# The opening of a fused gated-attention and token-mixer kernel: a z piece cast later, warm-up products, one block computed instead of turned, score pairs split between engines, loads at other times

## The chip, the cores and the metric

The kernel runs on one core of a Trainium2 chip. The time is that of one launch, in device microseconds, taken as the median of several runs; lower is better. A core has five engines that run their own instruction queues: TensorE (PE: matrix products; its weight loads are listed as PEld), VectorE (DVE), ScalarE (ACT), GpSimd (POOL) and SyncE (SP, which here only issues DMAs). They meet through semaphores. PSUM, the accumulator memory, has eight banks.

## What is computed

Two modules in a row, for each of 8 batches of 3200 tokens:

```
scores = z @ z.T / S                      # z: 3200 x 64
attn   = maximum(scores, 0) ** 2
x      = u * (attn @ v)                   # u, v: 3200 x 256

wq, wk = x @ w_q, x @ w_k                 # 256 x 64 each
mixed  = (wq @ wk.T / 8) @ x              # no softmax: wq @ (wk.T @ x)
out    = maximum(mixed, 0) @ w_out        # 256 x 256
```

Inputs and output are float32; the kernel multiplies in float16 and accumulates in float32.

## The kernel before

**Tiles.** A batch has 25 tiles of 128 tokens (the rows of scores) and seven groups of columns, six of 512 and one of 128. For each group the kernel makes the scores of all 25 tiles against the group's columns, squares their positive part, and accumulates the product with v in four PSUM banks (`acc00` to `acc11`; two halves of the group, two row halves of the product).

**Pairs.** Scores are made two tiles at a time (`use_pair`, `scores`): two products on the two row halves of the array, into one of two PSUM slots (`ps`). `first_stage` takes them out with a relu, on ACT or DVE, 1024 columns at once, into a float32 tile `g`; `second_stage` squares `g` into a float16 tile `at`, on ACT or POOL. There are 14 `at` buffers. The slot is free for a later pair, projection or other use when the relu is done.

**Blocks that are turned.** The score matrix is symmetric. For two groups near each other `is_turned` is true, and the block made for the earlier group is transposed by a DMA from SP (`turn`, tile `tt` or `ttl`) and used again for the later one, where no scores are made. An `at` buffer is free only when its turned blocks have been read.

**The order.** The program's order is made while it is built, by a scheduler with its own clocks for four engines (`clock`), for SP (`sp_at`) and for the DMA (`dma_at`). Its main loop takes, step by step, a pair of scores, an extra (projection, heads, mix, output) or one accumulation step (`acc_step`, `open_rows`), whichever its clocks find ready. `at_time` and `move` queue loads and DMAs for a planned time. `choose` and `squares` pick the engine of a relu and a square. Each engine then executes its queue in that order, waiting on semaphores: the planned times themselves are in no instruction, only the order is.

**The opening.** Batch 0's z comes in four pieces (`ZCH`: tiles 0 to 3, 12 to 17, 18 to 24, 4 to 11), is cast to float16 twice side by side (`cast_first`), turned by TensorE (`turn_first`) and copied to `zT`. v of batch 0 comes in five loads from POOL's queue (`load_first_v`), converted to float16 on the way. All four z pieces use buffers of the pool for x. The loads of u, of w_out and of the other weights follow on SP; nothing ahead of the first of them waits for a compute engine. The first pieces' casts are spread over DVE, ACT and POOL; those of the last piece are on POOL and DVE, and the DVE one is in the queue ahead of the first relu.

**Later.** When the two halves of a group are accumulated, `gate` takes them out of PSUM (ACT copy, DVE addition), multiplies with u on POOL, and SP transposes the result to `xT_sb` for the projections (L371), which accumulate toward `hs`. Mix (L436) and output products (L463) of a batch are placed among the next batch's accumulations. `batch_begun` plans the loads and transposes of the next batch's z and the loads of its v. The tail after the main loop ends the last batch.

Of the kernel before, what the change touches and what calls it, by code (L numbers as in the profile page):

```python
# [16 lines left out]
def kernel(  # L17
# [36 lines left out]
    NEARBY = 8  # L54

# [53 lines left out]
    def cast_first(c, parts=(0, 1)):  # L109
# [5 lines left out]
            (nc.gpsimd.tensor_copy, nc.vector.tensor_copy),  # L115
        ][c]
        for half, cast in enumerate(casts):
            if half in parts:
                cast(out=zd0[:, n0 : n0 + nn, half, :], in_=z32[n0][:])

    def turn_first(c):
        n0, nn = ZCH[c]
        tp = acc_tile(1 - c // 2, c % 2, "ztp", FP16)
# [4 lines left out]
        clock[PE] += 0.14 * nn  # L128
# [4 lines left out]
        z_at[c] = give(ACT if on_act else DVE, ready, 0.2 + 0.065 * nn)  # L133
# [38 lines left out]
    wo32 = {}  # L172

    def load_weights():
        wo32[0] = px.tile([P, ND, D], FP32, tag="x_sb", name="wo32")
        loads = [(wo32[0][:], moe_w_out.rearrange("(c p) e -> p c e", p=P))]
        for r in range(2):
            for w32, w in ((wq32, moe_w_q), (wk32, moe_w_k)):
                loads.append((w32[top(r), :, :], w.rearrange("(c p) h -> p c h", p=dh)))
        for half in range(2):  # L180
            loads.append((wk2[:, :, half, :], moe_w_k.rearrange("(c p) h -> p c h", p=P)))
        for i, (t, w) in enumerate(loads):
            move(18.0 + i, 26.0 + i, 0.65, 0.5, lambda t=t, w=w: nc.sync.dma_start(out=t, in_=w))

    def cast_weights():
# [3 lines left out]
        nc.gpsimd.tensor_copy(out=wo[:], in_=wo32[0][:])  # L189
# [3 lines left out]
    def is_turned(gi, gj):  # L193
# [4 lines left out]

    tiles, ends = [], {}
    for b in range(B):  # L200
        for gi in range(NG):
            near = [t for t in range(NT) if is_turned(gi, group_of(t))]
            own = [
                t for t in range(NT) if t not in near and not is_turned(group_of(t), gi)
            ]
            if b == 0 and gi == 0:
                order = own + near
# [30 lines left out]
    def first_stage(p, sc, on_act):  # L238
        g = pg.tile([P, 2, W], FP32, tag="g", name="g")
        for hs, w in pieces(p):  # L240
# [11 lines left out]
    def second_stage(p, g, on_act):  # L252
        at = pat.tile([P, 2 * W], FP16, tag="at", name="at")
        at0 = 0
        for hs, w in pieces(p):
# [8 lines left out]
        for tile_ in tiles[2 * p : 2 * p + 2]:  # L264
# [3 lines left out]
            if is_turned(gi, gj):  # L268
# [268 lines left out]
    keys_at, out_of, turned_at, z_at = {}, {}, {}, {}  # L537
# [50 lines left out]
    def cold():  # L588
        return 2.0 if clock[PE] < 11.0 else 1.0
# [9 lines left out]
    def use_pair():  # L599
# [12 lines left out]
    def squares():  # L612
        while pending and pending[0][0] <= clock[PE] + 0.3:
# [3 lines left out]
            done = give(ACT, ready, 1.06) if on_act else give(POOL, ready, 1.9)  # L617
            for (b, gi, gj, _, nn, _, _), turn in second_stage(p, g, on_act):
# [108 lines left out]

    def batch_begun(b, t):
        if b + 1 < B:
            t += 6 if b == 0 else 0  # L730
            at_time(t + 6, lambda: (load_z(b + 1), push(3.0)))
            for half in range(2):
                at_time(
                    t + 18 + 3 * half,
                    lambda half=half: (double_z(b + 1, half), give(DVE, clock[PE], 0.98)),
                )
            for i in range(5):
                move(t + 24 + 6 * i, t + 40 + 6 * i, 1.28, 1.05, lambda i=i: turn_z(b + 1, i))
            for i in range(5):
                at_time(t + 20 + 13 * i, lambda i=i: (load_v(b + 1, 5 * i, 5), push(2.5)))  # L740
# [43 lines left out]
    def open_rows():  # L784
# [8 lines left out]
        if b == 0 and gi == 0:  # L793
            ready = [t for t in ready if v_at[t] <= clock[PE]]
# [4 lines left out]
        if len(take) < want:  # L799
            if closing and len(left) - len(take) < 4:  # L800
                take = take[: len(left) - 4]
# [231 lines left out]
```

## Time and profile before

| | us |
|---|---|
| median of three runs | 787.96 (787.84 to 788.57) |
| the profiled execution | 789.18 |
| its span, first to last instruction | 787.2 |
| TensorE busy | 766.2 |
| POOL busy | 638.5 |
| ACT busy | 542.1 |
| DVE busy | 504.1 |

The profile is one execution. Its page gives the busy time of each engine, the chain of work that ended last, and groups of instructions by source line, with what the engine waited for ahead of them. Views of the trace give the same for any stretch of the span. Busy times of engines overlap; an engine's idle time counts only where the others have nothing to do meanwhile.

### The profile page before, as it was taken

How to read it: one execution, taken by the hardware profiler on the slowest of the kernel's cores; microseconds unless marked ns; L12 is line 12 of the kernel's file. 1: busy time of each engine (PE TensorE's matmuls, PEld its weight loads, DVE VectorE, ACT ScalarE, POOL GpSimd, SP SyncE). 2: the span in 40 equal slices, each digit the busy share in tenths (PEclk: the TensorE clock that was granted, in tenths of full speed). 3: DMA queues.
4: the chain of work that ended last, by engine and by line, in shares of the span. 5: the costliest groups of instructions: out<-in, count | busy, mean ns of one | idle time of the engine just before them, and what ended most of it. 6: DMA issues, size and time to landing. Idle time of an engine off the chain costs nothing.

```text
span 787.2 us, 28217 instructions
## 1 busy us (share of the span) xinstructions
PE 766.2 (97%) x12373; PEld 661.6 (84%) x12373; DVE 504.1 (64%) x514; ACT 542.1 (69%) x646; POOL 638.5 (81%) x524
## 2 busy tenths in 40 slices
PE   6989999999999999999998999999999999999996
PEld 4879999887899888988887887988879988898884
DVE  5655768564687566775575666777576665666635
ACT  5757678768687767867676765776667766777534
POOL 7969597887888877898687998789778788988961
PEclk9999999999999999999999999999999999999999
DMA  8999999999999999999989999999979999779616
GB/s 196 145 175 167 166 175 176 184 181 168 214 174 180 201 192 192 195 178 205 188 159 158 213 183 176 180 196 202 207 175 172 154 211 229 177 115 213 146 56 213
DMA packets 308522, 141.38 MB, mean 180 GB/s; under 512 B 287152, under 2 KB 290096, under 8 KB 308400
## 3 DMA queue, kind: packets, MB, share of 16 engines
q1 hardware_dynamic: 301488, 123.42, 83.2%
q0 software_dynamic: 6768, 15.98, 15.3%
q8 instruction: 96, 1.57, 0.8%
q14 instruction: 26, 0.21, 0.1%
q10 hardware_dynamic: 144, 0.20, 0.1%
HBM read 59.64 MB, written 26.21 MB: 109 GB/s over the span
## 4 chain that ended last, share of the span: by engine, by line
PE 91%; DMA 3%; DVE 2%; ACT 1%; issue 1%; POOL 0%; SPq 0%; DVEq 0%; POOLq 0%; ACTq 0%
PE acc L302 66%; PE sc L223 12%; PE fo L463 6%; PE qk L371 3%; DMA xT_sb<-x_sb 3%; PE qk L408 2%; PE mx L436 1%; DVE g L246 1%; DMA z<-in_z_dram 1%; POOL at L261 0%; ACT at L259 0%; ACT g L242 0%; DVE fo L486 0%; PE hd L408 0%; DVE both L319 0%
## 5 line engine op out<-in xcount | busy, mean ns | idle before, releaser
L302 PE MATMUL acc<-v_sb,at 64*128 64x256 f16 x7312 | 495.3, 270 | 3.4 <-ACT at L259 2.5
L261 POOL TENSOR_TENSOR at<-g 128x1024 f16<-128x1024 f32 (+1 forms) x244 | 449.3, 1854 | 56.8 <-DVE g L246 50.6
L246 DVE TENSOR_SCALAR g<-sc 128x1024 f32<-128x1024 f32 (+2 forms) x321 | 376.0, 1189 | 138.1 <-PE sc L223 133.0
L302 PEld LDWEIGHTS <-at 64*128 64x128 f16 x7312 | 399.7, 94 | 57.1 <-issue 7.7
L259 ACT ACTIVATE at<-g 128x1024 f16<-128x1024 f32 (+2 forms) x224 | 229.5, 1034 | 20.1 <-DVE g L246 17.7
L242 ACT ACTIVATE g<-sc 128x1024 f32<-128x1024 f32 x147 | 149.2, 1016 | 58.6 <-PE sc L223 56.2
L223 PE MATMUL sc<-zT 64*128 64x512 f16 x920 | 185.7, 378 | 3.3 <-DVE g L246 2.9
L340 POOL TENSOR_TENSOR x_sb<-both,u_sb 128x512 f16<-128x512 f32 (+1 forms) x112 | 134.5, 1207 | 57.5 <-DVE both L319 56.1
L302 PE MATMUL acc<-v_sb,tt 64*128 64x256 f16 x2304 | 159.6, 269 | 0.0
L302 PEld LDWEIGHTS <-tt 64*128 64x128 f16 x2304 | 125.2, 94 | 13.8
L319 DVE TENSOR_TENSOR both<-acc,both 128x512 f32<-128x512 f32 (+1 forms) x104 | 69.7, 670 | 92.6 <-ACT both L318 76.3
L318 ACT COPY both<-acc 128x512 f32<-128x512 f32 (+1 forms) x104 | 58.8, 567 | 81.7 <-PE acc L302 76.4
L223 PEld LDWEIGHTS <-zT 64*128 64x128 f16 x920 | 59.4, 94 | 14.1 <-issue 9.7
L491 ACT ACTIVATE fo<-fo 128x1024 f32<-128x1024 f32 (+1 forms) x48 | 44.5, 929 | 23.2 <-PE fo L463 22.9
L463 PE MATMUL fo<-wo,rt 128*128 128x256 f16 x400 | 53.0, 274 | 1.3 <-ACT rt L451 0.5
L453 ACT ACTIVATE rt<-mx 128x1024 f16<-128x1024 f32 (+1 forms) x49 | 45.7, 932 | 12.3 <-PE mx L436 12.1
L384 ACT CAST qk<-qk 128x512 f16<-128x512 f32 (+1 forms) x54 | 29.3, 543 | 34.5 <-PE qk L408 28.5
L463 PEld LDWEIGHTS <-rt 128*128 128x128 f16 x400 | 35.0, 98 | 15.9 <-issue 11.0
L423 DVE TENSOR_TENSOR ha<-qk,ha 128x512 f32<-128x512 f32 x37 | 25.6, 691 | 27.5 <-ACT qk L384 26.8
L371 PE MATMUL qk<-xT_sb,wqk 64*128 64x256 f16 (+1 forms) x404 | 32.2, 266 | 3.3 <-DMA xT_sb<-x_sb 3.3
L401 POOL COPY kx<-kx 128x128 f16<-128x128 f16 (+1 forms) x99 | 26.1, 291 | 7.5 <-DMA kx<-qk 7.5
L408 PE MATMUL qk<-x_sb,kx 64*128 64x256 f16 x342 | 27.9, 269 | 0.0
(44 smaller groups left out, 226.3 us busy)
## 6 DMA issues: line engine op xcount, KB each, us to landing
u_sb<-in_u_dram SPq DMA_DIRECT2D x48, 512.0 KB, 5.2
out_dram<-fo SPq DMA_DIRECT2D x47, 512.0 KB, 4.6
v_sb<-in_v_dram POOLq DMA_DIRECT2D x35, 320.0 KB, 6.0
zn<-in_z_dram POOLq DMA_DIRECT2D x7, 400.0 KB, 6.9
tt<-at SPq DMA_TRANSPOSE x144, 4.5
u_sb<-in_u_dram SPq DMA_DIRECT2D x8, 128.0 KB, 4.6
out_dram<-fo SPq DMA_DIRECT2D x8, 128.0 KB, 2.6
xT_sb<-x_sb SPq DMA_TRANSPOSE x56, 5.6
```

The costliest lines, as they stand in the source:

```text
L223: nc.tensor.matmul(out=sc[:, h, 0:gw], lhsT=zT[b][top(h), ts(ti, P)], rhs=zT[b][top(h), ds(gs, gw)], start=True, stop=True,)
L242: nc.scalar.activation(out=g[:, hs, 0:w], in_=sc[:, hs, 0:w], func=RELU, scale=GSCALE)
L246: nc.vector.tensor_scalar(out=g[:, hs, 0:w], in0=sc[:, hs, 0:w], scalar1=0.0, scalar2=GSCALE, op0=AOP.max, op1=AOP.mult,)
L259: nc.scalar.square(out=out, in_=g[:, hs, 0:w])
L261: nc.gpsimd.tensor_mul(out=out, in0=g[:, hs, 0:w], in1=g[:, hs, 0:w])
L302: nc.tensor.matmul(out=accs[half, r][:, ds((j % 2) * D, D)], lhsT=weights(b, gi, ti, j)[top(r), :], rhs=vs[b][top(r), ti, :], start=(first ...
L318: nc.scalar.copy(out=both[:, 0 : n * D], in_=accs[half, 0][:, 0 : n * D])
L319: nc.vector.tensor_add(out=both[:, 0 : n * D], in0=accs[half, 1][:, 0 : n * D], in1=both[:, 0 : n * D])
L340: nc.gpsimd.tensor_mul(out=xs[b, gi][:, 0:n, :, r, :].rearrange("p n c d -> p (n c) d"), in0=both[:, 0 : n * D].rearrange("p (m d) -> p m ...
L371: nc.tensor.matmul(out=ps[:, r, 0 : n * P], lhsT=wqk[top(r), c, :, :].rearrange("p t h -> p (t h)"), rhs=xTs[b, gi][top(r), 0:n, c, :], st ...
L453: nc.scalar.activation(out=out, in_=ps[:, 0:nr, 0 : ND * n * P], func=RELU)
L463: nc.tensor.matmul(out=banks[r][:, ds(j * D, D)], lhsT=flat[:, ds((dc * n + j) * P, P)], rhs=wo[:, dc, :], start=(dc == 0 and j == 0), sto ...
```

## The change

- z pieces three and four are loaded into buffers of the pool for u, not into those for x. The first two loads of u use the same buffers, so on SP they now wait until these pieces have been cast.
- v of batch 0: one load of tiles 0 to 3 in place of two of two tiles each; the loads that follow are issued after POOL's casts.
- 28 products of the identity with itself stand on TensorE ahead of the first transposes, and five after the third piece's. Nothing reads their result.
- Both casts of the last z piece are on DVE, and stand behind the first relus. Its transposes write to a score slot and stand behind the first accumulations.
- The tiles of batch 0's group 0 are ordered by the z piece that they come from.
- In batch 0 the block of groups 0 and 2 is not turned: group 2 makes its scores itself.
- Until the planned time 24 a pair may be split: one tile's relu on ACT and the other's on DVE, and one tile's square on ACT and the other's on POOL.
- w_out is loaded and cast later and into another buffer, w_k's second copy later; v of batch 1 is planned from 56 in steps of 11, in place of 38 in steps of 13; batch 1's z transposes in steps of 4 in place of 6.
- The scheduler's own starting clocks, its v times and the time for which it takes TensorE as slow are others. So the order of all later work changes as well. Accumulations of later batches wait, in its plan, for their v.

```diff
     def load_first_z():
         for i, (n0, nn) in enumerate(ZCH):
-            z32[n0] = px.tile([P, nn, dqk], FP32, tag="x_sb", name="z32")
+            pool, tag = (px, "x_sb") if i < 2 else (pu, "u_sb")
+            z32[n0] = pool.tile([P, nn, dqk], FP32, tag=tag, name="z32")
...
-    def cast_first(c, parts=(0, 1)):
+    def cast_first(c):
...
-            (nc.gpsimd.tensor_copy, nc.vector.tensor_copy),
+            (nc.vector.tensor_copy, nc.vector.tensor_copy),
         ][c]
...
     def turn_first(c):
         n0, nn = ZCH[c]
-        tp = acc_tile(1 - c // 2, c % 2, "ztp", FP16)
+        if c < 3:
+            tp = acc_tile((c + 1) // 2 % 2, c % 2, "ztp", FP16)
+        else:
+            open_slot()
+            tp = pps.tile([P, 4 * W], FP16, tag="ps", name="ztp")
...
+    def warm(n):
+        for _ in range(n):
+            nc.tensor.matmul(out=idle[:, 0:P], lhsT=ident[:], rhs=ident[:], start=True, stop=True)
+        clock[PE] += 0.053 * cold() * n
...
         for half in range(2):
-            loads.append((wk2[:, :, half, :], moe_w_k.rearrange("(c p) h -> p c h", p=P)))
...
+            move(110.0, 130.0, 0.65, 0.4, lambda t=t, w=w: nc.sync.dma_start(out=t, in_=w))
...
+        move(76.0, 80.0, 0.65, 0.8, lambda: nc.sync.dma_start(out=wo32, in_=w))
+        at_time(40.0, cast_weights)
+        at_time(90.0, lambda: (nc.gpsimd.tensor_copy(out=wo[:], in_=wo32), give(POOL, 0.0, 0.6)))
...
+    SKIP = [(0, 2)]
+
+    def is_turned(b, gi, gj):
+        if b == 0 and (gi, gj) in SKIP:
+            return False
         return gi < gj and (gj <= gi + FAR or gj == LASTG)
...
             if b == 0 and gi == 0:
-                order = own + near
+                order = sorted(range(NT), key=lambda t: (first_chunk(t), t))
...
     def use_pair():
...
-        on_act = choose(*(max(clock[x], ready) for x in (ACT, DVE)))
-        done = give(ACT, ready, 1.03) if on_act else give(DVE, ready, 1.2)
-        g = first_stage(p, sc, on_act)
+        a, d = (max(clock[x], ready) for x in (ACT, DVE))
+        if clock[PE] < UNTIL and max(a + 0.57, d + 0.68) + SPLIT < min(a + 1.03, d + 1.2):
+            ways = [a < d, a >= d]
+            done = max(give(ACT, ready, 0.57), give(DVE, ready, 0.68))
+        else:
+            ways = [choose(a, d)]
+            done = give(ACT, ready, 1.03) if ways[0] else give(DVE, ready, 1.2)
+        g = first_stage(p, sc, ways)
...
     def batch_begun(b, t):
         if b + 1 < B:
-            t += 6 if b == 0 else 0
-            at_time(t + 6, lambda: (load_z(b + 1), push(3.0)))
+            t0 = max(t + 6, Z0)
+            at_time(t0, lambda: (load_z(b + 1), push(3.0)))
...
             for i in range(5):
-                at_time(t + 20 + 13 * i, lambda i=i: (load_v(b + 1, 5 * i, 5), push(2.5)))
+                at = t + 20 + 13 * i if b else V0 + V1 * i
+                at_time(at, lambda i=i: v_loaded(b + 1, 5 * i, 5))
...
     make_identity(nc, ident)
     load_first_z()
-    load_first_v(0, 2)
+    load_first_v(0, 4)
+    idle = acc_tile(0, 1, "warm")
+    warm(28)
     cast_first(0)
     cast_first(1)
-    load_first_v(2, 2)
     cast_first(2)
     load_first_v(12, 6)
-    cast_first(3, [0])
     load_first_v(18, 7)
     load_first_v(4, 8)
-    clock[:] = [4.5, 4.95, 4.7, 7.8]
-    v_at = [4.5] * 2 + [8.2] * 2 + [18.7] * 8 + [11.2] * 6 + [14.7] * 7
+    clock[:] = [4.4, 4.75, 4.3, 7.0]
+    for t, n0, nn in ((7.0, 0, 4), (18.0, 4, 8), (10.5, 12, 6), (14.0, 18, 7)):
+        v_at.update({(0, n): t for n in range(n0, n0 + nn)})
     dma_at[0] = 16.0
     turn_first(0)
-    cast_first(3, [1])
-    give(DVE, 0.0, 0.65)
     turn_first(1)
     current.update(b=0, gi=0, left=list(range(NT)), fresh=True)
     groups.pop(0)
     use_pair()
     use_pair()
     turn_first(2)
-    turn_first(3)
+    warm(5)
+    at_time(8.6, lambda: (cast_first(3), give(DVE, 8.6, 0.86)))
+    at_time(10.0, lambda: turn_first(3))
```

`UNTIL` is 24.0, `SPLIT` 0.2, `Z0` 24, `V0` 56, `V1` 11. `second_stage` and `squares` are changed like `first_stage` and `use_pair`.

More of the change, by code (lines that the diff above doesn't have):

```diff
@@ L54 @@
     NEARBY = 8
+    KEEP = 4
     consts = ctx.enter_context(tc.tile_pool(name="consts", bufs=1))
@@ L616, in squares @@
             on_act = a + SPARE < c and (a + 1.06 <= shut() + LATE or a + 2.5 < c)
[L617 to L618 removed]
+            ways = [on_act]
+            if clock[PE] < UNTIL and max(a + 0.57, c + 0.97) + SPLIT < min(a + 1.06, c + 1.9):
+                ways = [a < c, a >= c]
+                done = max(give(ACT, ready, 0.57), give(POOL, ready, 0.97))
+            else:
+                done = give(ACT, ready, 1.06) if on_act else give(POOL, ready, 1.9)
+            for (b, gi, gj, _, nn, _, _), turn in second_stage(p, g, ways):
                 n = nn * widths[gi] // P
```

86 lines of the change are left out of this document (57 added, 29 removed).

## The prediction

> **What bounds the kernel now.** I read the page first, then busy time by stretches of the span, then the waits of TensorE, then the chain of waits and the timeline of the opening. From the page:
>
> ```profile
> span 787.2 us, 28217 instructions
> ...
> PE 766.2 (97%) x12373; PEld 661.6 (84%) x12373; DVE 504.1 (64%) x514; ACT 542.1 (69%) x646; POOL 638.5 (81%) x524
> ...
> PE 91%; DMA 3%; DVE 2%; ACT 1%; issue 1%; POOL 0%; SPq 0%; DVEq 0%; POOLq 0%; ACTq 0%
> ...
> L371 PE MATMUL qk<-xT_sb,wqk 64*128 64x256 f16 (+1 forms) x404 | 32.2, 266 | 3.3 <-DMA xT_sb<-x_sb 3.3
> ```
>
> TensorE is busy for 97% of the span and 91% of the chain that ends last runs through it, so a saving counts only where TensorE stands still or runs at half clock. Busy time by stretches (columns: length, then busy time of PE, PEld, DVE, ACT and POOL, granted clock, DMA share, GB/s) says where that is:
>
> ```profile
> 4.40:14.70 10.30, 7.73 (x68) 5.16 (x70) 5.95 (x8) 6.58 (x8) 7.76 (x9) 0.83 1.05 251
> ...
> 25.00:30.00 5.00, 4.29 (x69) 3.48 (x67) 3.30 (x5) 4.97 (x8) 4.98 (x4) 1.00 0.86 153
> ...
> 40.00:50.00 10.00, 9.54 (x165) 8.95 (x163) 4.63 (x5) 5.61 (x7) 6.81 (x5) 1.00 1.23 140
> 50.00:58.00 8.00, 5.13 (x70) 3.59 (x66) 5.41 (x5) 5.22 (x6) 5.68 (x4) 1.00 1.10 220
> ...
> 180.00:200.00 20.00, 18.95 (x311) 15.67 (x308) 9.03 (x10) 15.29 (x21) 14.72 (x13) 1.00 1.06 179
> ...
> 400.00:440.00 40.00, 37.75 (x624) 32.79 (x622) 24.85 (x26) 28.11 (x33) 33.15 (x27) 1.00 1.04 156
> 440.00:760.00 320.00, 320.00 (x5224) 273.58 (x5220) 207.41 (x209) 218.75 (x261) 270.80 (x216) 1.00 0.94 181
> 760.00:787.20 27.20, 20.64 (x252) 15.25 (x246) 14.57 (x19) 11.07 (x21) 5.64 (x5) 0.97 0.44 155
> ```
>
> From 440 to 760 us TensorE never stands still at full clock. The losses are the opening (68 matmuls in 10.3 us, granted clock 0.83), 0.71 us at 25 to 30, 0.46 and 2.87 us between 40 and 58, and two single waits at 180 to 200 and 400 to 440. The change edits the first 100 us alone, so the sum consists of what it does to the first four, plus what it displaces later. What TensorE waits for between 25 and 60 us:
>
> ```profile
> PE sc L223 <- DVE g L246: 2.9, 4, 1.1
> PE acc L302 <- DVE both L319: 0.8, 2, 0.5
> PE sc L223 <- ACT g L242: 0.4, 1, 0.4
> ```
>
> The 3.3 us (2.9 and 0.4) are score products waiting for the relu two pairs before them to empty one of two PSUM slots: TensorE had run out of accumulations and had only scores left to make.
>
> **The opening, part by part.** Its chain of waits before (start, length, what):
>
> ```profile
> 6.08 0.43 DVE zd L119
> ...
> 7.64 1.15 DVE zT L132 x2
> ...
> 9.96 1.06 ACT at L259
> ...
> 11.05 1.03 PE acc L302 x8
> 12.08 0.43 PE sc L223 x2
> ...
> 14.98 0.22 PE sc L223 x2
> ...
> 18.68 1.20 PE acc L302 x22
> ```
>
> The last z piece's cast (6.08) and two zT copies sit ahead of relus on VectorE, and the first accumulation starts at 11.05. A pair of score products then takes 0.43 us, at 14.98 only 0.22: the clock fell during the idle time ahead of 11.05. The named releaser there, ACT's square, is not the real one. In the program order the first accumulation uses ACT's first square and the second v load. From the timeline:
>
> ```profile
> 1.44 0.72 POOL L107 DMA_DIRECT2D v_sb<-in_v_dram  x1
> ...
> 4.13 0.53 POOL L107 DMA_DIRECT2D v_sb<-in_v_dram  x1
> ...
> 4.66 0.57 POOL L119 CAST zd<-z 128x448 f16<-128x448 f32 x1
> ...
> 5.63 1.04 PE L223 MATMUL sc<-zT 64*128 64x512 f16 x4
> ...
> 7.76 1.06 ACT L259 ACTIVATE at<-g 128x1024 f16<-128x1024 f32 x1
> ```
>
> and from the DMA issues of 0 to 30 us (count, KB each, us from issue to landing):
>
> ```profile
> u_sb<-in_u_dram SPq DMA_DIRECT2D x2, 512.0 KB, 7.0
> v_sb<-in_v_dram POOLq DMA_DIRECT2D x1, 512.0 KB, 10.9
> v_sb<-in_v_dram POOLq DMA_DIRECT2D x1, 448.0 KB, 8.7
> ...
> v_sb<-in_v_dram POOLq DMA_DIRECT2D x1, 384.0 KB, 8.1
> v_sb<-in_v_dram POOLq DMA_DIRECT2D x2, 128.0 KB, 6.8
> ```
>
> That square ended at 8.82; the second v load landed at 4.13 + 6.8 = 10.93. So v held it. The change loads v tiles 0 to 3 at once at 1.44, and u's two loads, 512 KB each, now wait on SP for the buffers of the third and fourth z pieces. For 256 KB I have 6.8 us (128 KB) and 8.1 (384 KB), so it lands between 8.2 and 9.5 by these rows, sooner if the held-back u matters; I take 8.2, as the u loads leave the engines free just then.
>
> The other durations, grouped by shape over 4 to 30 us (busy, mean ns):
>
> ```profile
> L261 POOL TENSOR_TENSOR at<-g 128x1024 f16<-128x1024 f32 x9 | 16.8, 1896 | 3.4 <-DVE g L246 3.4
> L246 DVE TENSOR_SCALAR g<-sc 128x1024 f32<-128x1024 f32 x12 | 14.3, 1220 | 6.2 <-PE sc L223 6.2
> ...
> L259 ACT ACTIVATE at<-g 128x1024 f16<-128x1024 f32 x10 | 10.5, 1056 | 0.8 <-DVE g L246 0.6
> ...
> L319 DVE TENSOR_TENSOR both<-acc,both 128x512 f32<-128x512 f32 x2 | 1.4, 692 | 1.7 <-ACT both L318 1.7
> ...
> L318 ACT COPY both<-acc 128x512 f32<-128x512 f32 x2 | 1.2, 592 | 0.0
> ...
> L132 DVE COPY zT<-ztp 128x896 f16<-128x896 f16 x1 | 0.6, 625 | 0.0
> ...
> L119 DVE CAST zd<-z 128x512 f16<-128x512 f32 x1 | 0.4, 428 | 0.6 <-DMA z<-in_z_dram 0.6
> ```
>
> Half pairs do not occur. Their nearest rows are 512 wide: ACT 0.59, DVE 0.69, POOL half of 1.90 = 0.95. In the changed order pair 0 is split between ACT and DVE, and its square between POOL and ACT. The first scores come at 5.63 as before. DVE copies zT piece 1 (about 0.6), so its half relu ends near 6.95; ACT's half starts near 5.85 (5.63 + 0.22) and ends near 6.45. POOL casts piece 2 until 5.23, issues three v loads at 0.53 each (until 6.83), and squares its half by 7.8. First accumulation: the later of 7.8 and v's 8.2.
>
> After 12 accumulations (22 take 1.20 us in the same chain, 0.055 each, so 0.66) the order has one score pair (0.22), two accumulations and then the transposes of piece 3. These wait for DVE: copy of piece 2 (6.95 + 0.62), relu of pair 2 (+1.22), both casts (2 × 0.43) = 9.65, and eight transposes end near 10.1. This is what the deferral costs: TensorE stands about half a microsecond for the casts, and behind the transposes in its queue stand all further accumulations. Before, at 14.7, six pairs and 32 accumulations were done. The change has 18 accumulations and one pair left at 10.1, so reaches the same state at 10.1 + 0.98 + 0.22 = 11.3: 3.4 us ahead.
>
> Two things take from that. Tile 12's v: issued near the same 5.2 and landed at 13.3 before (5.16 + 8.1). Unchanged, it would hold TensorE 2.0 us; with about half of u and all of wo out of its way it lands earlier. I take 11.5, which costs 0.2; the bounds are 0 and 2.0. And the engines: until group 0 ends the order gives ACT 20 halves and 5 whole instructions, 20 × 0.59 + 5 × 1.04 = 17.0 us from 5.85, that is until 22.9, just when TensorE would end the group. I charge 0.5. So the opening gains 2.7 us, bounds 0.9 and 3.4.
>
> **The clock.** Before, the 4.4 to 14.7 stretch was granted 0.83. The 28 warm-up products (and five later) use an otherwise idle TensorE and an accumulation bank that nothing needs yet, so they cost nothing while they end before z's casts; afterwards each would cost about 0.1 (a quarter of the 0.43 that 512 columns took at half clock). In the Trainium skill, "TensorE: Matmul & The Clock Gate", Part 1 says that about 3.4 us of sustained work opens the gate and that a cold 128-column product starts every 106.7 ns. By it 28 of them last 3.0 us, not quite enough, and the first ten transposes stay at half clock: an estimate of 0.5 us less gain, 782.9. No run here shows warm-ups yet. By the rows I have the first scores no earlier than before (5.63), so the sum doesn't need it.
>
> **The 40 to 58 us stretch.** Here the order counts. Before, the tightest run of eight successive score pairs has 24 accumulations between first and last, and that is this stall. In the changed order, past the opening, the tightest has 86. One relu takes 1.22 us on DVE and ACT shares them, so eight pairs need about 4 to 5 us; 24 accumulations (1.3 us) plus seven pairs (1.5) do not cover that, 86 (4.7) plus 1.5 do. Weights, v of batch 1 and the unturned block free SP and DMA there. I take the whole 3.3 us; the bounds are 0 (the wait moves) and 3.3. The two waits for the group's eviction (0.8) stay, bounds 0.8 either way.
>
> **Added and moved work.** Block (0,2) not turned: two transposes fewer on SP, four score products (two pairs) more: 2 × 0.22 = 0.44 us on TensorE, plus two relus and squares on engines that have room after 30 us. u(0,0) is first read at group 0's gate (past 23 us), far behind a landing near 5.3 + 7.0 = 12.3; the second u waits on SP until 9.65 and nothing behind it on SP is ready before the first squares to be turned. wo and the second wk load go later, far ahead of the first projection and of the ending. If this cover failed, a late u would cost the gate, not TensorE, up to its two spare buffers. v of batch 1 comes in five loads from 56 to 100 us instead of 38 to 90, still ahead of batch 1's start past 100. I cost these at 0.
>
> **Sum.** 2.7 + 3.3 - 0.44 = 5.6 us. The profiled execution took 789.18 us around its span of 787.2; the median of three runs is 787.96. Against the former 783.6, against the median, which I forecast, **782.4 us**.
>
> **Rivals.** All later order is shuffled too, since the scheduler places everything by one clock.
>
> *Late xT.* The two single waits, 1.05 and 2.25 us, are projections for xT:
>
> ```profile
> DMA to landing us min/median/max: 2.3/5.6/11.2
> ```
>
> These are 56 transposes with a median of 5.6 us; the two that took above 10 stalled TensorE, 3.3 us together, 1.65 each. If the new order meets busy DMA (share over 1 until 440 us) at five more group ends, it costs 8.2: 790.6, slower than before. It decides from the fourth extra wait (5.6 / 1.65). Against it: 320 us without one after 440. Chance 0.07, and 0.04 for three or four, no change. Conversely both vanish: 782.4 - 3.3 = 779.1, chance 0.10.
>
> *The 50 us stall only moves* to another place in batch 0, because squares' buffers stay as many: 782.4 + 3.3 = 785.7. The order of 86 speaks against it, the DMA share of 1.1 to 1.2 for it. Chance 0.15.
>
> *The opening starts earlier but waits for v again* (the change doesn't do what it says): v at 13.3 as before gives 0.9 instead of 2.7, 784.2. DMA was saturated (1.05) in that stretch with or without u. Chance 0.14.
>
> **Numbers.** My forecast has 0.50. The range of 778.5 to 786.8 takes in both xT waits gone and either opening or middle gain failing; it leaves out about 0.15. A measurement here can tell about 0.2% (1.6 us) from no change. Faster 0.88: all cases but the slow ones and a joint failure of opening and middle; same 0.05; slower 0.07.
>
> **What would show it.** Right: first accumulation near 8.2, the seventh pair's state near 11.3 to 12, granted clock 1.00 by 10 us, no score waits above 0.5 us at 35 to 60, and the 440 to 760 stretch still full. Wrong: v landing past 12; TensorE waiting on DVE's casts for more than a microsecond near 9; new idle time at qk's products in later batches.

## The result, and the profile after

| | median, us | lowest to highest | runs |
|---|---|---|---|
| before, same chip | 788.36 | 785.53 to 793.17 | 22 |
| after | 784.50 | 782.43 to 793.13 | 22 |

The ratio is 0.9957, with a 95% interval of 0.9938 to 0.9977: of 788.36 us that is 3.4 us less, between 1.8 and 4.9. The forecast was 5.6 us less. The profiled execution of the changed kernel took 784.44 us. The page after:

```profile
span 782.7 us, 28343 instructions
...
PE 769.8 (98%) x12410; PEld 663.7 (85%) x12410; DVE 503.3 (64%) x515; ACT 546.4 (70%) x663; POOL 645.1 (82%) x530
...
PE 92%; DVE 2%; DMA 1%; ACT 1%; POOL 1%; issue 1%; DVEq 0%; SPq 0%; ACTq 0%
```

Against the profile of before the span is 4.5 us shorter, and TensorE is busy 3.6 us longer. The 33 warm-up products take as much (3.17 and 0.44 us), most of it in time that was idle before. Where the time came from is seen in stretches (length; busy time of PE, PEld, DVE, ACT, POOL; granted clock; DMA share; GB/s). After:

```profile
4.40:14.70 10.30, 7.99 (x94) 5.16 (x94) 7.85 (x12) 5.95 (x10) 8.32 (x9) 1.00 0.98 196
14.70:25.00 10.30, 9.53 (x146) 7.73 (x144) 8.04 (x10) 8.63 (x15) 8.88 (x8) 1.00 0.71 130
25.00:30.00 5.00, 4.54 (x72) 3.52 (x68) 3.95 (x6) 4.46 (x7) 3.66 (x4) 1.00 0.64 144
40.00:50.00 10.00, 9.80 (x170) 9.28 (x167) 5.83 (x8) 5.71 (x7) 8.78 (x10) 1.00 1.15 183
50.00:58.00 8.00, 7.92 (x128) 6.94 (x125) 5.83 (x6) 6.49 (x8) 8.00 (x5) 1.00 1.12 164
58.00:760.00 702.00, 700.91 (x11463) 607.80 (x11460) 450.71 (x456) 495.33 (x589) 592.89 (x481) 1.00 1.00 181
```

and two stretches of before that the prediction did not show:

```profile
14.70:25.00 10.30, 10.30 (x172) 8.99 (x168) 7.62 (x7) 7.35 (x8) 9.00 (x6) 1.00 0.74 98
58.00:760.00 702.00, 698.54 (x11434) 606.72 (x11430) 456.50 (x462) 493.35 (x584) 587.08 (x476) 1.00 1.02 181
```

Between 40 and 58 us TensorE now idles 0.28 us, where it idled 3.33. Past 58 us it idles 1.09 in place of 3.46. But from 14.7 to 25 us it was full before and now stands still for 0.77 us. It also gets less done there: 146 matrix products in place of 172. What it waits for in the whole span (engine, line, releaser; us in total, times, longest):

```profile
PE ztp L130 <- DVE zd L120: 1.0, 1, 1.0
PE hd L438 <- POOL kx L431: 0.9, 1, 0.9
PE sc L247 <- DVE g L273: 0.8, 3, 0.4
PE sc L247 <- ACT g L269: 0.8, 3, 0.3
PE acc L332 <- DMA v_sb<-in_v_dram: 0.7, 1, 0.7
```

Neither the score waits of 2.9 us at 50 to 58 nor the waits for xT (3.3 us before) are left. Of the score waits before, 0.4 us (ACT's) lay at 27.5 us, not past 40, and 0.3 us of it is still there. The first, the third and the fifth wait and 0.5 us of the fourth are new and lie in the opening. Its timeline after (start, length, what, and in brackets the idle time ahead of it and its releaser):

```profile
5.65 1.03 PE L247 MATMUL sc<-zT 64*128 64x512 f16 x4
...
8.11 0.89 PE L332 MATMUL acc<-v_sb,at 64*128 64x256 f16 x12
...
9.24 1.59 DVE L120 CAST zd<-z 128x512 f16<-128x512 f32 x2
...
9.41 2.33 POOL L291 TENSOR_TENSOR at<-g 128x512 f16<-128x512 f32 x2 [0.39 <-DVE g L273]
...
10.90 0.62 PE L130 MATMUL ztp<-ident,zd 128*128 128x128 f16 x8 [1.01 <-DVE zd L120]
...
12.44 0.38 PE L332 MATMUL acc<-v_sb,at 64*128 64x256 f16 x4
...
13.52 0.50 PE L332 MATMUL acc<-v_sb,at 64*128 64x256 f16 x6 [0.70 <-DMA v_sb<-in_v_dram]
...
15.65 0.39 PE L247 MATMUL sc<-zT 64*128 64x512 f16 x2 [0.32 <-ACT g L269]
...
26.10 1.28 ACT L348 COPY both<-acc 128x512 f32<-128x512 f32 x2
```

The first accumulation starts at 8.11 us instead of 11.05, and six pairs and 32 accumulations (12 + 2 + 14 + 4) are done at 12.82 instead of 14.7. Then the lead melts: group 0's sum is taken out of PSUM from 26.10 us; before, the same copy came at

```profile
26.02 0.59 ACT L318 COPY both<-acc 128x512 f32<-128x512 f32 x1
```

This copy ("the read-out") is the mark of the opening used below. By it the opening gained nothing.

### The profile page after: what moved, and what is told of

It reads as the page before. It is cut to its first block, busy times and chain, and to the rows that moved or that the text cites. A ratio compares the mean times of both kernels' runs of the same rounds, so it can differ in the third digit from the quotient of the medians.

```text
span 782.7 us, 28343 instructions
## 1 busy us (share of the span) xinstructions
PE 769.8 (98%) x12410; PEld 663.7 (85%) x12410; DVE 503.3 (64%) x515; ACT 546.4 (70%) x663; POOL 645.1 (82%) x530
## 4 chain that ended last, share of the span: by engine, by line
PE 92%; DVE 2%; DMA 1%; ACT 1%; POOL 1%; issue 1%; DVEq 0%; SPq 0%; ACTq 0%
PE acc L332 67%; PE sc L247 13%; PE fo L493 6%; PE qk L401 3%; PE qk L438 2%; PE mx L466 1%; DVE g L273 1%; DMA v_sb<-in_v_dram 1%; POOL at L291 1%; ACT g L269 1%; ACT at L289 0%; DMA z<-in_z_dram 0%; DVE fo L516 0%; PE hd L438 0%; DVE both L349 0%
## 5 line engine op out<-in xcount | busy, mean ns | idle before, releaser
L291 POOL TENSOR_TENSOR at<-g 128x1024 f16<-128x1024 f32 (+2 forms) x252 | 457.1, 1827 | 62.4 <-DVE g L273 50.3
L269 ACT ACTIVATE g<-sc 128x1024 f32<-128x1024 f32 (+2 forms) x159 | 156.5, 986 | 67.1 <-PE sc L247 58.5
L247 PE MATMUL sc<-zT 64*128 64x512 f16 x924 | 187.6, 377 | 1.9 <-DVE g L273 0.8
L332 PEld LDWEIGHTS <-tt 64*128 64x128 f16 x2272 | 123.5, 94 | 14.3
L453 DVE TENSOR_TENSOR ha<-qk,ha 128x512 f32<-128x512 f32 x37 | 25.6, 691 | 30.7 <-ACT qk L414 30.2
```

What stands on the lines that cost most here:

```text
L247: nc.tensor.matmul(out=sc[:, h, 0:gw], lhsT=zT[b][top(h), ts(ti, P)], rhs=zT[b][top(h), ds(gs, gw)], start=True, stop=True,)
L269: nc.scalar.activation(out=g[:, hs, 0:w], in_=sc[:, hs, 0:w], func=RELU, scale=GSCALE)
L291: nc.gpsimd.tensor_mul(out=out, in0=g[:, hs, 0:w], in1=g[:, hs, 0:w])
L332: nc.tensor.matmul(out=accs[half, r][:, ds((j % 2) * D, D)], lhsT=weights(b, gi, ti, j)[top(r), :], rhs=vs[b][top(r), ti, :], start=(first ...
```

## The experiments

Each edit is against the changed kernel unless it says "before". The runs were made on several chips, each beside runs of the kernel before, so kernels are compared by the ratio and not by the medians. Score waits are TensorE's, between 25 and 60 us.

| kernel | ratio to before (95%) | median, us | read-out, us | pairs ahead of it, halved relus | TensorE busy 14.7 to 25 (of 10.30) |
|---|---|---|---|---|---|
| before | | 787.96 | 26.02 | 17, 0 | 10.30 |
| before, second profile | | (784.53, one) | 24.53 | 17, 0 | 10.30 |
| after | 0.9957 (0.9938 to 0.9977) | 784.50 | 26.10 | 17, 16 | 9.53 |
| turned again | 0.9966 (0.9944 to 0.9987) | 784.89 | 25.95 | 17, 16 | 9.53 |
| loads back | 0.9991 (0.9958 to 1.0024) | 786.64 | 25.76 | 17, 16 | 9.47 |
| u late | 0.9982 (0.9965 to 1.0000) | 785.94 | 25.73 | 17, 16 | 9.39 |
| u early | 0.9967 (0.9948 to 0.9986) | 784.83 | 25.59 | 17, 16 | 9.39 |
| no warm-ups | 1.0060 (1.0028 to 1.0093) | 793.62 | 26.01 | 18, 12 | 9.55 |
| short lead | 1.0013 (0.9986 to 1.0040) | 789.97 | 24.89 | 15, 16 | 9.82 |
| casts on ACT | 0.9945 (0.9918 to 0.9972) | 783.63 | 26.28 | 18, 8 | 9.81 |
| whole pairs | 0.9960 (0.9944 to 0.9977) | 783.83 | 26.93 | 17, 0 | 10.30 |
| whole pairs, casts on ACT | 1.0007 (0.9985 to 1.0029) | 788.71 | 23.89 | 16, 0 | 10.30 |
| before + block not turned | 1.0026 (0.9994 to 1.0057) | 788.76 | 29.70 | 19, 0 | 9.11 |
| before + loads moved | 0.9982 (0.9953 to 1.0011) | 786.39 | 27.29 | 17, 0 | 10.30 |

Pairs are the relus ahead of the read-out in each trace, two halves counted as one pair; the fifth column gives also how many relus are halves.

**Which edit empties the 40 to 58 us stretch?** First the block of groups 0 and 2 turned again:

```diff
-    SKIP = [(0, 2)]
+    SKIP = []
```

> The changed kernel with one part undone: the block of groups 0 and 2 of batch 0 is turned again. Theory M1 (the gain lies in the 40 to 60 us stretch and comes from not turning this block, whose two extra score pairs fill TensorE's time and free at buffers): the score waits on relu between 40 and 60 us come back, 2 to 3.5 us of them, the third group's read-out falls back toward 57.8, and the time is 2.5 to 3.5 us above the changed kernel's. Rival M2 (the loads moved out of this stretch did it): no score wait above 0.5 us there, and the time is that of the changed kernel less 0.4 for the two pairs saved.

The stretch stayed free of the old stall (TensorE busy 9.80 of 10 and 7.18 of 8 us) and the time is that of the changed kernel within its interval. So with the loads moved the unturned block isn't needed, as the rival had said. The other way round, loads of wo, wk and of batch 1's v and z as before:

```diff
-            move(110.0, 130.0, 0.65, 0.4, lambda t=t, w=w: nc.sync.dma_start(out=t, in_=w))
+            move(22.0 + half, 30.0 + half, 0.65, 0.4, lambda t=t, w=w: nc.sync.dma_start(out=t, in_=w))
...
-        move(76.0, 80.0, 0.65, 0.8, lambda: nc.sync.dma_start(out=wo32, in_=w))
+        move(18.0, 26.0, 0.65, 0.8, lambda: nc.sync.dma_start(out=wo32, in_=w))
...
-        at_time(90.0, lambda: (nc.gpsimd.tensor_copy(out=wo[:], in_=wo32), give(POOL, 0.0, 0.6)))
+        at_time(41.0, lambda: (nc.gpsimd.tensor_copy(out=wo[:], in_=wo32), give(POOL, 0.0, 0.6)))
...
-    V0 = 56
-    V1 = 11
+    V0 = 38
+    V1 = 13
...
-            step = 6 if b else 4
+            step = 6
```

> The changed kernel with the load times undone: w_out and the second w_k early again, batch 1's v from 38 in steps of 13, z's transposes in steps of 6; block (0,2) stays unturned. Theory R (either edit alone clears the 40 to 60 us stretch, as the turned-block run left it clear with the loads moved): no more than 1 us of score waits between 25 and 60 us, time within 1 us of the changed kernel's. Rival M2 (the moved loads alone did it): 2 to 3.5 us of score waits return there.

A score wait of 1.0 us for DVE came back, not 2.9 (the 0.3 for ACT at 27 us is the changed kernel's own). That lies between the two expectations, and so does the time: the ratio is 0.9991 against 0.9957, and the intervals overlap. (A wait of 1.0 of the same kind is also in the profile with u late, below, where these loads were not touched; so this one is no proof against them.) Then each edit alone on the kernel before. The block alone:

```diff
-    def is_turned(gi, gj):
+    def is_turned(b, gi, gj):
+        if b == 0 and (gi, gj) == (0, 2):
+            return False
```

> The kernel before with one part of the change alone: block (0,2) not turned. Theory R: the 3.3 us of score waits at 40 to 58 us are gone, two more pairs cost 0.44, so about 2.9 us below the kernel before, ratio 0.996. Rival M2: the waits stay and the ratio is 1.000 or a little above.

```profile
7.75 0.43 DVE L119 CAST zd<-z 128x512 f16<-128x512 f32 x1 [2.46 <-DMA z<-in_z_dram]
...
29.70 0.59 ACT L320 COPY both<-acc 128x512 f32<-128x512 f32 x1 [0.75 <-PE acc L304]
```

Those are two rows of its timeline. The 50 to 58 us stretch is full (8.00 of 8.00), as expected, but the time is not better: in this run the last z piece came at 7.75 instead of 6.08, the order has 19 pairs ahead of the read-out, and that slipped to 29.70. The loads alone:

```diff
-            loads.append((wk2[:, :, half, :], moe_w_k.rearrange("(c p) h -> p c h", p=P)))
+            move(110.0, 130.0, 0.65, 0.4, lambda t=t, w=w: nc.sync.dma_start(out=t, in_=w))
...
+        move(76.0, 80.0, 0.65, 0.8, lambda: nc.sync.dma_start(out=wo32, in_=w))
+        at_time(40.0, cast_weights)
+        at_time(90.0, lambda: (nc.gpsimd.tensor_copy(out=wo[:], in_=wo32), give(POOL, 0.0, 0.6)))
...
-                at_time(t + 20 + 13 * i, lambda i=i: (load_v(b + 1, 5 * i, 5), push(2.5)))
+                at_time((t + 20 + 13 * i) if b else 56 + 11 * i, lambda i=i: (load_v(b + 1, 5 * i, 5), push(2.5)))
```

> The kernel before with one part of the change alone: w_out and the second w_k loaded later, w_out into the other buffer, batch 1's v from 56 in steps of 11. Theory R: the score waits at 40 to 58 us are gone or below 0.7 us, time 3 to 3.7 us below the kernel before, ratio 0.995 to 0.996, which is the whole effect of the change. Rival M1 (the block is needed): the waits stay above 2 us, ratio 0.999 or above.

No wait for DVE's relus is left; 0.4 us for ACT's is, ahead of 38 us. 50 to 58 us is full. The time, 786.39, is not told apart from before, nor from the gain that was expected; its profile is of the slowest of its ten executions (793.24). So on the kernel before either edit alone removes the stall, and neither alone gives a gain that these runs resolve.

**Does a landing hold the opening?** u's loads behind v's instead of beside them, then u's loads not held back at all:

```diff
-        if gi + 1 < NG:
+        if (b, gi) == (0, 0):
+            move(21.0, 25.0, 0.55, 1.6, lambda: load_u(b, gi + 1))
+        elif gi + 1 < NG:
...
-    move(10.0, 14.0, 0.55, 1.6, lambda: load_u(0, 0))
+    move(19.0, 18.0, 0.55, 1.6, lambda: load_u(0, 0))
```

> The changed kernel with the first two u loads behind the first turned block on SP (past 18 us), so v has the DMA engines to itself from about 8 us. Theory V (v's late landing, at 13.5, 17.5 and 20.7 us, sets the opening): v's second load lands by 11.5, the 0.7 us wait for it is gone and group 0's read-out comes at 24 to 25 us in place of 26.1. Theory P (the relu and square chain sets it): the loads land earlier too, but the read-out stays within 0.5 us of 26.1.

```diff
-            pool, tag = (px, "x_sb") if i < 2 else (pu, "u_sb")
+            pool, tag = px, "x_sb"
```

> The changed kernel with all four z pieces in buffers of the pool for x, so that the two u loads start at about 2 us as in the kernel before. Theory V: v's third and fourth loads land again at about 15.6 and 18.3 us in place of 17.5 and 20.7, the second one no earlier than 13; group 0's read-out 0 to 1 us sooner. Theory P: the read-out stays within 0.5 us of 26.1 whatever v does. z's last piece lands before 7.7 or at it.

With u late, the three later v loads took 7.4, 9.0 and 11.0 us instead of 8.6, 12.1 and 14.8, and the 0.70 us wait for v was gone. With u early the first accumulation waited for v until 9.57, 1.46 us later than in the changed kernel. Yet the read-outs are 25.73 and 25.59: v 1.2 us sooner gave 0.4, where 1 to 2 were expected of it, and a start 1.5 us later did not delay the end but stood beside one 0.5 us sooner. So v's landing does not set the read-out alone. The second run by itself would not decide: 25.59 is 0.01 us outside what the one theory allows and inside what the other does.

**What does the split of pairs cost?** All pairs whole:

```diff
-    UNTIL = 24.0
+    UNTIL = 0.0
```

> The changed kernel with no pair split (relus and squares whole from the start). Theory P (from 14 to 26 us the relu and square chain sets the pace, and splitting makes it dearer: ACT's 20 halves at 0.60 for 10 wholes at 1.03): ACT and DVE are less busy in this stretch and group 0's read-out comes at 25 to 26 us, no later than the 26.1 of the changed kernel. Rival S (splitting is what lets the first pairs through sooner, as it was meant to): first accumulation at 9 us or later in place of 8.1, group 0's read-out at 27 us or later, time 1 us or more above the changed kernel's.

```profile
7.46 3.93 POOL L291 TENSOR_TENSOR at<-g 128x1024 f16<-128x1024 f32 x2 [1.07 <-DVE g L273]
...
9.00 2.67 DVE L120 CAST zd<-z 128x512 f16<-128x512 f32 x2
```

The read-out fell between the two expectations (26.93). These rows of its timeline say why: POOL squares whole pairs beside these casts, and they take 2.67 us for the two. TensorE waited 2.2 us for them and its granted clock fell (0.89, then 0.95 from 14.7 to 25 us). The first accumulation came at 8.40, so the split brings it only 0.3 us sooner (8.11). The time was no worse than the changed kernel's, against what the theory that splitting pays had forecast. So the casts were moved to ACT, with pairs split as before:

```diff
-            (nc.vector.tensor_copy, nc.vector.tensor_copy),
+            (nc.scalar.copy, nc.scalar.copy),
...
-    at_time(8.6, lambda: (cast_first(3), give(DVE, 8.6, 0.86)))
+    at_time(8.6, lambda: (cast_first(3), give(ACT, 8.6, 1.2)))
```

> The changed kernel with the two casts of z's last piece on ScalarE in place of VectorE. Theory C (VectorE's casts took 0.42 and 1.26 us because GpSimd squares at the same time; alone such a cast took 0.43): on ScalarE each takes about 0.6, as its casts of 256 and 384 columns took 0.40 and 0.51, and the GpSimd half squares under way come down from 1.17 to 1.0 us. ScalarE is the fuller engine, so group 0's read-out stays within 0.7 us of 26.1 and the time within 1 us. Rival: the casts are as slow on ScalarE, 1 us or more, because the late landing of z (7.7 us) or SBUF is what slows them.

```profile
9.35 1.14 ACT L120 CAST zd<-z 128x512 f16<-128x512 f32 x2
```

The two casts took 1.14 us together (each 0.63, the second beginning 0.1 us ahead of the first one's end), POOL squaring beside them; its whole square took 1.89 us, as it does with no cast beside it. So theory C held for the casts. The read-out is no sooner (26.28, with 18 pairs ahead of it). At 783.63 this has the lowest median, but its interval and the changed kernel's overlap almost wholly. Both edits together:

```diff
-    UNTIL = 24.0
+    UNTIL = 0.0
...
-            (nc.vector.tensor_copy, nc.vector.tensor_copy),
+            (nc.scalar.copy, nc.scalar.copy),
...
-    at_time(8.6, lambda: (cast_first(3), give(DVE, 8.6, 0.86)))
+    at_time(8.6, lambda: (cast_first(3), give(ACT, 8.6, 1.2)))
```

> The changed kernel with whole pairs and with the casts of z's last piece on ScalarE: the two parts that made the opening's relus, squares and casts dearer are undone, the rest stays. Theory P with C: the casts end by 10 in place of 11.6 (whole pairs, VectorE), the half-clock stretch that the whole-pair run had at 11 to 14 us is gone with the wait for them, and group 0's read-out comes at 24.5 to 25.5, before the 26.1 of the changed kernel and the 26.9 of whole pairs alone. Rival S (splitting is needed): read-out at 26.5 or later. The time: 0.5 to 1.5 us below the changed kernel's by the opening, if later waits do not differ; these may differ by more than that in any one run.

Timeline, and TensorE's waits of the same kernel:

```profile
23.89 0.59 ACT L348 COPY both<-acc 128x512 f32<-128x512 f32 x1
```

```profile
PE qk L401 <- POOL wqk L205: 2.8, 2, 2.4
```

The earliest read-out of all, 2.2 us ahead of the changed kernel's. The time shows nothing of it: the projections then come so soon that they wait 2.8 us for the weights' casts on POOL, TensorE works 6.71 of the 10 us from 40 on, and its clock falls to 0.71 there. The expectation held for the read-out, which came still earlier than said, though the casts ended at 10.66 and not by 10; it failed for the time, whose ratio is 1.0007 against 0.9957.

**Fewer pairs ahead of the accumulations.** `lead` is how far, in accumulation steps, the scheduler runs ahead with scores; it is 140.

```diff
-        wanted = able and p * total < (done_acc + lead) * NPAIR
+        wanted = able and p * total < (done_acc + (60 if now < 24.0 else lead)) * NPAIR
```

> The changed kernel with score pairs made less far ahead until the planned time 24 (60 accumulation steps in place of 140): 15 in place of 17 pairs stand ahead of group 0's end in TensorE's order. Theory P (the relus and squares of the pairs made in group 0 set when it ends, at about 1.1 us a pair from the first scores on): group 0's read-out comes 1.5 to 2.5 us earlier than 26.1, at 23.6 to 24.6. Rival L (a latency within the chain of waits, or v's last load at 20.7, sets it): within 0.7 us of 26.1. In both, the time stays within 1 us of the changed kernel's, because the pairs left out are made in group 1.

15 pairs ahead of the read-out brought it to 24.89, just outside the nearer of the two bounds. It was paid back at once: TensorE worked 2.78 of the 5 us from 25 to 30 and 7.48 of 10 from 40 to 50, with 2.5 us of waits for the weights' casts. By the ratios the time was some 4 us worse than the changed kernel's, which no theory had said.

**The warm-ups.** Both calls left out:

```diff
-    idle = acc_tile(0, 1, "warm")
-    warm(28)
...
-    warm(5)
```

> The changed kernel without its 33 warm-up products. Theory P (relus and squares set group 0's end, TensorE has room): the first transposes and scores run at half clock either way, group 0's read-out stays within 0.7 us of 26.1, and so does the time within 1 us. Rival W (the clock is needed): TensorE still at half clock past 8 us, or falling back to it in its waits before 14 us, read-out 1.5 us or more later.

In its profile the read-out is no later, at 26.01, and the granted clock is 1.00, as theory P had said. The first four scores run at half clock with and without warm-ups (1.03 us for the four in both profiles), so there the 28 did not serve them; the first accumulation comes at 9.50 in place of 8.11. But its runs take 789.31 to 799.87 us, where theory P had the time within 1 us. The scheduler charges the warm-ups, so without them the later order differs, and in the profiled execution TensorE idles 0.96 us at 40 to 50, 1.33 at 58 to 180 and 2.29 at 440 to 760. That is the fastest of the ten executions; the others' granted clock over the span is lower (0.991 to 0.996, against 0.999). Why they take up to 10 us more is open.

**The kernel before, once more**, unchanged, to see how much of its first profile is its own.

> The kernel before, unchanged, profiled once more. Theory Z (its opening hangs on the landing of z's last piece, which two kernels with the same opening order showed at 6.9 and 7.8 us in place of 6.05, with group 0's read-out at 27.3 and 29.7 in place of 26.0): the read-out follows the landing, about 1.5 us for each us that z is late. Rival N (the opening is the same in every run): z within 0.3 us of 6.05 and read-out within 0.3 us of 26.0.

Stretches, TensorE's waits and one row of the timeline of this second profile:

```profile
4.40:14.70 10.30, 8.33 (x91) 5.68 (x91) 7.24 (x9) 7.22 (x8) 8.51 (x10) 1.00 1.06 249
...
50.00:58.00 8.00, 5.13 (x70) 3.57 (x67) 6.21 (x6) 5.81 (x7) 6.49 (x4) 1.00 1.10 228
58.00:760.00 702.00, 701.84 (x11500) 611.93 (x11498) 457.73 (x465) 494.12 (x585) 588.63 (x477) 1.00 1.00 181
```

```profile
PE sc L223 <- DVE g L246: 2.9, 4, 1.1
PE acc L302 <- DMA v_sb<-in_v_dram: 2.0, 1, 2.0
...
PE qk L371 <- DMA xT_sb<-x_sb: 0.5, 1, 0.5
```

```profile
24.53 0.59 ACT L318 COPY both<-acc 128x512 f32<-128x512 f32 x1
```

The stall of 2.9 us and the 5.13 of 8 us at 50 to 58 are there again, to the tenth. The rest is not: the clock stays at 1.00 through the opening and the read-out comes 1.5 us sooner; past 58 us TensorE idles 0.16 us, not 3.46, and xT costs 0.5, not 3.3. This execution took 784.53 us, as little as the changed kernel's median. Neither expectation held: z's last piece landed 0.3 us sooner, which by the one theory gives 0.4, and by the other the read-out should not have moved.

## Why the time came out inside the range though the opening's term failed

| step, as predicted | forecast | after |
|---|---|---|
| first accumulation | 8.2 us | 8.11 |
| last z casts end | 9.65 | 10.83 |
| TensorE stands for them | 0.5 us | 1.01 |
| six pairs and 32 accumulations | 11.3 | 12.82 |
| wait for v's tile 12 | 0.2 us | 0.70 |
| opening's gain | 2.7 us (0.9 to 3.4) | none at the read-out |
| 40 to 58 us | 3.3 us | 3.33 idle to 0.28 |
| later waits (xT) | unchanged | 3.46 idle to 1.09 |

**The middle stretch was right**, in place and mechanism. The reason that the prediction gives, too few accumulations between score pairs, can be counted in the order of each trace: the fewest accumulations between the first and the last of eight successive pairs, from 38 to 60 us, beside TensorE's waits for relus there (counted from the matmul records).

| profiles | fewest accumulations | waits for relus, us |
|---|---|---|
| before, both | 24 | 2.87 |
| u late | 54 | 1.02 |
| loads back | 70 | 1.01 |
| before + block not turned | 86 | 0 |
| after; u early | 92 | 0.08 |
| before + loads moved; short lead | 96 | 0 |
| whole pairs; no warm-ups | 98 | 0 |
| turned again | 104 | 0.39 |
| whole pairs, casts on ACT | 104 | 0 |
| casts on ACT | 122 | 0 |

So the moved loads and the unturned block work through the same cause: each alone, on the kernel before, spreads the pairs from 24 to 86 and 96 accumulations. The size was nearly right. The 3.3 of the sum counts 0.4 us of waits at 27.5 us, of which 0.3 stayed; the fall from 3.33 to 0.28 is 2.8 us of relu waits and 0.26 of a wait for the eviction, which was to stay. The fall of 3.05 less the 0.44 reckoned for two pairs is 2.6, inside the measured 1.8 to 4.9. That this is most of the measured gain follows from the sum; no run shows it by the time alone.

**The releaser of the first accumulation was right.** The second profile of before names the v load (2.0 us) where the first named ACT's square. In the four profiles with before's opening the accumulation starts 0.13 to 0.14 us after that load's landing. In the changed kernel the 8.2 came true with the roles exchanged: v landed at 7.84, and POOL's half square, forecast for 7.8, ended at 8.02 and came last. That is luck.

**The opening's term failed**, and with it the lower bound of 0.9. Three steps of it were too small. *The casts* were costed at 2 × 0.43 from a row with no square of POOL beside it. In the changed kernel they took 0.42 and 1.26, which its row shows when it is grouped by line (shortest, middle and longest in ns; first and last start):

```profile
L120 DVE CAST zd<-z x2: 418/840/1261, 9.2 to 9.6; 128x512 f16<-128x512 f32 x2
```

The second cast began at 9.58, while POOL made a half square (9.41 to 10.56), and ended at 10.84, 0.28 us after that square. With whole pairs (the two rows in that experiment) POOL's square ended at 11.39 (7.46 + 3.93) and the cast at 11.67 (9.00 + 2.67), again 0.28 us later. So a cast that begins while POOL squares costs what is left of the square. The casts also began 0.45 us later than forecast (9.24 in place of 8.79), for the reason given under the engines. With both the state came at 12.82, 1.5 late. *The v tile* landed 2 us later than assumed, at 13.5. This is the condition of the rival that waits for v again (13.3), but not its price: TensorE came there late itself and waited 0.70, not 2.0.

*The engines*, costed at 0.5 by adding up ACT's instructions alone, took most. The prediction lets ACT and DVE work on the two halves of a pair at the same time (pair 0: ends near 6.45 and 6.95). In the trace they work one behind the other: ACT from 6.30 to 6.90, DVE from 6.93 to 7.62, and two later pairs:

```profile
10.76 0.68 DVE L273 TENSOR_SCALAR g<-sc 128x512 f32<-128x512 f32 x1
...
11.47 0.60 ACT L269 ACTIVATE g<-sc 128x512 f32<-128x512 f32 x1 [1.19 <-DVE g L273]
...
12.65 0.60 ACT L269 ACTIVATE g<-sc 128x512 f32<-128x512 f32 x1
...
13.28 0.69 DVE L273 TENSOR_SCALAR g<-sc 128x512 f32<-128x512 f32 x1 [1.03 <-ACT g L269]
```

In none of the 63 split relus of the eight kernels with halves do the two overlap; in 56 of them the profile names the first half as what the second waited for, and the second starts within 0.04 us of its end. Both halves write one tile `g` and read one slot; which of the two makes them wait was not taken apart. (The halves of a square do overlap: POOL 9.41 to 10.56, ACT 9.64 to 10.28.) Relus by shape, 5.6 to 24 us (busy, mean ns; idle ahead of them and what ended it), before:

```profile
L246 DVE TENSOR_SCALAR g<-sc 128x1024 f32<-128x1024 f32 x9 | 10.7, 1220 | 5.5 <-PE sc L223 5.5
...
L242 ACT ACTIVATE g<-sc 128x1024 f32<-128x1024 f32 x6 | 6.1, 1019 | 4.9 <-PE sc L223 4.9
```

and after:

```profile
L273 DVE TENSOR_SCALAR g<-sc 128x512 f32<-128x512 f32 x8 | 5.4, 686 | 2.8 <-ACT g L269 2.5 <-PE sc L247 0.3
L269 ACT ACTIVATE g<-sc 128x512 f32<-128x512 f32 x8 | 4.8, 595 | 6.0 <-DVE g L273 4.3 <-PE sc L247 1.6
```

Before, the engines idled until TensorE brought scores: TensorE set the pace and was full from 14.7 to 25 us. After, the halves idle behind one another, 4.3 and 2.5 us, and TensorE waits for slots. A half costs 0.60 and 0.69 us, so a split pair holds its slot for some 1.3 us and takes both engines in turn, against 1.02 or 1.22 for a whole relu on one engine that leaves the other to the next pair. Every kernel with halves has TensorE under 9.9 of 10.30 us there; of those without, only the kernel before with the unturned block does, where z's last piece came 1.7 us later than in before. Whole pairs with casts on ACT are the test: TensorE full again, the engines idle for scores again, and the read-out at 23.89. One pair of the 17 was missing there, worth some 1.2 us (20.5 us from the first scores to the read-out over 17); the other 1.0 of the 2.2 is the split and the casts together. How much is each was not taken apart. These are single profiles; the five kernels that keep the changed kernel's halves and casts (after, turned again, loads back, u late, u early) lie between 25.6 and 26.1, so one execution and another hardly make 2.2.

So the lead of 1.9 us at the sixth pair was given back to v (0.7) and to relus that came late: from 14.7 to 25 us TensorE finished 146 products in place of 172, some 1.6 us of work at the pace of before (10.30 × 26 / 172, an estimate), of which 0.77 shows as idle time. The last run of accumulations ends a quarter of a microsecond behind before's (24.30 + 2.47 = 26.77 us in the timeline, before's at 24.60 + 1.92 = 26.52).

**"Unchanged" was wrong for xT**, and was luck both ways. The sum stood on one execution of before in which two late transposes cost 3.3 us and a half-clock stretch cost the opening up to 1.5; the second profile has almost none of it. Past 58 us, TensorE's idle time ranges from 0.2 to 6.4 us over the fourteen profiles, with no part of the change to sort them by.

**What the nearness of the number is worth.** The forecast was 782.4 and 784.50 was measured, beside the 784.2 of the rival whose price did not come true. The time is in the range because the range left room for an opening that gains nothing. Of the prediction's signs of being wrong, two came: v past 12 us, and more than a microsecond of waiting for DVE's casts.

By these runs, the 5.6 should have read 0 + 3.05 - 0.44 = 2.6 us, give or take the waits that the reshuffled order brings: 785.4 us, against 784.50 measured. The 0 holds against the first profile of before. Against the second, with its read-out at 24.53, the opening's term is a loss of 1.6 us, and the changed kernel's profiled execution is only 0.1 us shorter than that one. How often the kernel before runs as in the one or the other, two profiles can't say.

## What to carry to other kernels

An earlier start is worth what is left of it at the next point where everything must have arrived: forecast that point (here the first read-out), and for a stage that hands work through several engines add up what each item holds, not only the busy time of one engine. Before items are halved between two engines, make sure that the halves run at once: here they ran one behind the other, which brought the first accumulation 0.3 us forward and cost throughput on all that followed. Count the order, too: where eight score pairs had the fewest accumulations between them, the stall was longest (24: 2.9 us, 54 and 70: 1.0, from 86 on 0 to 0.4). Profile the kernel before twice before single waits go into a sum: what is in both (the 2.9 us stall) belongs to the order, the rest to the execution.

## What the runs showed of the hardware

- A VectorE cast of 128x512 from float32 to float16 took 0.43 us beside a POOL cast. Ten such casts, in eight kernels, began while POOL squared; each ended 0.28 us after the end of that square. A cast that began early in the square thus took 1.26 us beside a half square and 2.11 beside a whole one. POOL's half squares lengthened as well, from 1.04 to 1.15 or 1.22 us, and the whole one from 1.89 to 2.07. VectorE's relus, which read PSUM, took 1.22 to 1.23 us with and without a square beside them. Two casts on ACT took 1.14 us together, and the square beside them 1.89. The Trainium skill, "GPSIMD Engine Reference", section "Specifications", says that GpSimd shares its SBUF interfaces with VectorE and contends with VectorE instructions in a two-port mode or with two SBUF inputs; the traces agree that the two hold each other up, and no run here shows in which mode the cast runs.
- The clock of one and the same program differs between executions. After an idle time of 2.5 us the first accumulations of before ran at half clock in one profile (eight in 1.03 us), after 2.0 us at full clock in the other (0.61). 28 warm-up products (3.17 us) were followed by four half-clock scores (1.03 us) in the changed kernel and by full-clock ones with casts on ACT (0.60), where TensorE's queue up to there is the same. The Trainium skill, "TensorE: Matmul & The Clock Gate", Part 1, explains such differences with an activity window of some 3.4 us that runs freely, so that the same kernel meets it at another phase each time; the rows agree, and its 3.4 us also fits that 3.17 us were not always enough. In these two profiles the granted clock of the stretch from 4.4 us read 1.00, so the products' own length was the surer sign.
